# When the second layer's 64-bit weights are converted, and which engine rounds the second expert weights

## The chip, the cores and the metric

One core of one Trainium2 chip runs the whole program. The metric is the time of one execution in device microseconds (us). The engines that matter here are TensorE (PE: matrix products and transposes), VectorE (DVE), ScalarE (ACT), GpSimd (POOL) and SyncE (SP), which issues nearly all transfers. Each engine works through its own instructions strictly in the order in which the program lists them; they meet only through semaphores.

## The reference

```python
attn_out = _attn_ref(q, k, v)               # 2 x 8 heads, 1152 keys, queries averaged in pairs
x = attn_out.transpose(0, 2, 1, 3).reshape(1152, 512)
...
for e in range(8):                          # each token goes to one expert
    mask = expert_idx == e
    h = np.maximum(x[mask] @ w1[e], 0.0)    # 512 -> 1024
    out[mask] = gate_w[mask, None] * (h @ w2[e])
...
a = x @ w_a                                 # 512 -> 1536
b = x @ w_b
return (a * b @ w_out).astype(np.float32)
```

The arrays `w_a`, `w_b` and `w_out` of the last layer, the second layer, arrive as 64-bit floats; everything else is 32-bit. [...]

## The kernel before

The program has three stages: attention (to about 285 us), the experts (to about 466 us) and the second layer (to the end). For accuracy every matrix product is made of three: each operand is split into a high part (rounded to the matrix engine's format) and a low part (what the rounding left), and high x high, high x low and low x high are added.

**The expert stage** is a loop over steps m = 0 to 34. Steps 0 to 15 serve the first half of the tokens, 16 to 31 the second half; `ORDER` gives the sequence. A step handles a quarter of the hidden units of one expert slot; a slot has one tile of 128 tokens or two. In the second half the sequence is a a b a b a b b A A B A B A B B, where a and A have two tiles, b and B one. The one-tile steps are therefore 18, 20, 22, 23, 26, 28, 30 and 31. `moe_step(m)` writes into the queues, in this order: the evictions of what the PE made before (`x_ev`; `h_ev2(m-2)` for one-tile steps; `h_ev(m-1)`), the first product `s1(m)` on the PE, the transposes `h_tr(m-1)` of a one-tile step, the split of the first weights of the next step `split1(m+1)` (ACT makes `w1h`, DVE makes `w1l`), the split of the second weights `split2(m-1)` and `split2b(m-1)` (high part `w2h` by ACT where m-1 is in `W2_ACT`, else by DVE; the two halves of the low part `w2l` mostly by POOL), the second product `s2(m-2)`, and the loads of weights for later steps (SP, three buffers each for first and second weights). For a one-tile step the second product needs `hl`, the low part of the hidden values, which DVE writes in `h_ev2`: it stands in the DVE's queue at the head of the step in which the PE needs it.

**The second layer's weights** come in 18 pieces of 1 MB. `weights` and `convert` are a generator that each later step moves on by one stage. If a piece begins at step m, then SP loads `raw` at m; ACT makes `cvt` (`Abs`, line 1057) at m+3; DVE runs four instructions (lines 1059, 1060, 1061 and 1063) at m+4; ACT rounds it to `wh` and POOL makes the first half of `wl` at m+5; POOL makes the second half at m+6. These stand at the end of their step, behind `moe_step(m)`, and so in front of everything of step m+1. `raw` and `cvt` have two buffers each. `W_AT` lists the steps at which the first six pieces begin; they are called C1 to C6 here. `W_AT2` does the same for the other twelve, at later steps of the second layer. C1 and C2 are needed by the first product `f1(0)` of the second layer, which stands ahead of step 32 on the PE; C3 by `f2(0)`, C4 and C5 by `f1(2)`, C6 by `f2(2)`.

Before the change the DVE's four instructions of C1 to C6 stand at the ends of steps 23, 25, 28, 31, 32 and of the first round of the second layer. The attention's tiles are released before step 17, and the second layer's tiles (`raw` among them) take their place in the memory.

Of the kernel before, what the change touches and what calls it, by code (L numbers as in the profile page):

```python
# [42 lines left out]
SETUP_AT, ROUTE_AT = 26, 43  # L43
ROUND1, P2_AT, DS = 3, 4, (1, 2, 1, 2, 1)
CONV_LAG, Y_LAG = 3, 4
W_AT = (19, 21, 24, 27, 28, 31)
W_AT2 = range(3, 27, 2)
W2_ACT = (1, 2, 3, 4, 5, 6, 7, 8, 9, 10, 12, 13, 16, 17, 18, 19, 21, 22, 24, 25, 27, 28, 31)
Y_AT, YB_AT = 20, 34
XALL_AT = 53  # L50
ORDER = ('aabababbAABABABB', 'aabababbAABABABB')
# [8 lines left out]
def fused(ctx, tc, q, k, v, emb, tau, w1, w2, wa, wb, wo, out):  # L60
# [3 lines left out]
    def copy_hi(dst, src, engine=None):  # L64

        if engine is nc.vector:
            nc.vector.tensor_copy(dst, src)
        else:
            nc.scalar.activation(out=dst, in_=src, func=AF.Copy)  # L69

    def sub_lo(dst, src, hi, engine=None):

        (engine or nc.vector).tensor_tensor(out=dst, in0=src, in1=hi.bitcast(F32), op=ALU.subtract)  # L73
# [780 lines left out]
    def split2(m):  # L854
        w = M[m].pop("w2r")
        h, l = M[m]["w2"] = [moe.tile([P, 2, DM], F32R, name=f"w2{x}") for x in "hl"]
        copy_hi(h, w, None if m in W2_ACT else nc.vector)
        sub_lo(l[:, 0], w[:, 0], h[:, 0], nc.vector if m in W2_DVE[0] else nc.gpsimd)
# [227 lines left out]
    def advance(start):  # L1086
        if start and todo:
            running.append(weights(*todo.popleft()))
        for g in list(running):
            if next(g, "end") == "end":  # L1090
                running.remove(g)
# [35 lines left out]
    def drive():  # L1127

        if yq:
            moving.append(ytrans(*yq.popleft()))  # L1130
        for g in list(moving):
            if next(g, "end") == "end":
                moving.remove(g)
# [53 lines left out]
    while m < NM + 3:  # L1187
# [7 lines left out]
        if m >= Y_AT:  # L1195
            drive()
        advance(m in W_AT)
        m += 1
# [141 lines left out]
```

## Time and profile before

| | us |
|---|---|
| median of 3 runs | 700.35 (699.89 to 703.0) |
| the profiled execution | 699.06 |
| its span, first to last instruction | 697.4 |

| engine | busy us | share of the span |
|---|---|---|
| PE | 617.9 | 89% |
| DVE | 494.7 | 71% |
| ACT | 372.6 | 53% |
| POOL | 317.3 | 46% |

The mean granted clock of the PE over the execution is 0.945 of full speed. In the chain of work that ended last, PE has 49% of the span, DVE 20%, DMA 5%, ACT 4%, POOL 3%. The shares are averages over three stages with different limits; what a change in the expert stage is worth is read from that stage's own stretch.

### The profile page before, as it was taken

How to read it: one execution, taken by the hardware profiler on the slowest of the kernel's cores; microseconds unless marked ns; L12 is line 12 of the kernel's file. 1: busy time of each engine (PE TensorE's matmuls, PEld its weight loads, DVE VectorE, ACT ScalarE, POOL GpSimd, SP SyncE). 2: the span in 40 equal slices, each digit the busy share in tenths (PEclk: the TensorE clock that was granted, in tenths of full speed). 3: DMA queues.
4: the chain of work that ended last, by engine and by line, in shares of the span. 5: the costliest groups of instructions: out<-in, count | busy, mean ns of one | idle time of the engine just before them, and what ended most of it. 6: DMA issues, size and time to landing. Idle time of an engine off the chain costs nothing.

```text
span 697.4 us, 13210 instructions
## 1 busy us (share of the span) xinstructions
PE 617.9 (89%) x5253; PEld 555.6 (80%) x5253; DVE 494.7 (71%) x790; ACT 372.6 (53%) x512; POOL 317.3 (46%) x233
## 2 busy tenths in 40 slices
PE   8588979888976875998999988969999999999996
PEld 6477768777865765898888876859999999999995
DVE  4978989889899875458867598974445575665523
ACT  3868887987856664345546575435342324223210
POOL 3958878787665543233414567674011212212100
PEclk8879999999988796999999999989999999999999
DMA  8979899999886589995789987445011313211012
GB/s 285 267 176 225 212 210 238 209 238 226 191 220 153 139 196 235 270 332 188 249 270 302 360 305 246 164 143 174 1 60 61 121 61 106 77 62 60 1 46 94
DMA packets 210051, 125.04 MB, mean 179 GB/s; under 512 B 156216, under 2 KB 181816, under 8 KB 209984
## 3 DMA queue, kind: packets, MB, share of 16 engines
q1 hardware_dynamic: 208512, 119.41, 62.8%
q0 software_dynamic: 1472, 4.72, 1.9%
q8 instruction: 43, 0.70, 0.4%
q14 instruction: 24, 0.20, 0.1%
HBM read 72.11 MB, written 13.67 MB: 123 GB/s over the span
## 4 chain that ended last, share of the span: by engine, by line
PE 49%; DVE 20%; DMA 5%; ACT 4%; issue 4%; POOL 3%; SPq 0%; ACTq 0%; DVEq 0%; POOLq 0%
PE ps_s L1147 21%; DVE nm L377 4%; PE ps_s L872 4%; PE ps_o L1169 4%; PE ps_m L1169 3%; PE ps_y L1169 3%; PE ps_s L372 2%; PE ps_o L443 2%; DVE vl L260 2%; DMA w2r<-in_moe_w_dram 2%; DMA eT<-ehl 2%; POOL w2l L73 2%; PE ps_o L915 1%; DMA xr<-xbuf 1%; ACT ehl L394 1%
## 5 line engine op out<-in xcount | busy, mean ns | idle before, releaser
L403 POOL TENSOR_TENSOR ehl<-e,ehl 128x1152 f16<-128x1152 f32 x61 | 147.8, 2424 | 75.3 <-ACT ehl L394 33.9
L73 POOL TENSOR_TENSOR wl<-cvt,wh 128x512 fp32r<-128x512 f32 x36 | 50.5, 1420 | 147.9 <-ACT wh L69 144.3
L382 ACT ACTIVATE e<-ps_s,nm 128x1152 f32<-128x1152 f32 x72 | 87.8, 1220 | 38.4 <-DVE nm L377 28.8
L377 DVE TENSOR_REDUCE nm<-ps_s 128x1 f32<-128x1152 f32 x72 | 97.1, 1349 | 12.8 <-PE ps_s L372 12.5
L73 POOL TENSOR_TENSOR w2l<-w2r,w2h 128x512 fp32r<-128x512 f32 x42 | 63.7, 1532 | 91.3 <-ACT w2h L69 51.7
L372 PE MATMUL ps_s<-kTh,qT 64*128 64x512 f32 (+2 forms) x480 | 98.4, 399 | 2.5 <-issue 1.0
L443 PEld LDWEIGHTS <-eT 128*128 128x128 f16 x1944 | 78.3, 103 | 23.9 <-issue 12.9
L443 PE MATMUL ps_o<-vh,eT 128*128 128x65 f16 (+1 forms) x1278 | 82.0, 204 | 16.1 <-DVE x L466 10.3
L372 PEld LDWEIGHTS ps_s<-kTh,qT 64*128 64x128 f32 x480 | 74.2, 206 | 8.8 <-issue 2.4
L443 PE MATMUL ps_o<-vl,eT 128*128 128x65 f16 (+1 forms) x639 | 76.7, 204 | 0.0
L394 ACT ACTIVATE ehl<-e 128x1152 f16<-128x1152 f32 (+1 forms) x65 | 72.3, 1112 | 0.2 <-DMA eT<-ehl 0.2
L1157 DVE TENSOR_TENSOR asb<-ps_s,asb 128x384 f32<-128x384 f32 x36 | 19.9, 554 | 69.1 <-PE ps_s L1147 69.1
L69 ACT ACTIVATE abh<-asb 128x384 fp32r<-128x384 f32 x36 | 18.9, 524 | 83.0 <-DVE asb L1157 83.0
L1152 ACT ACTIVATE asb<-ps_s 128x384 f32<-128x384 f32 x36 | 17.8, 493 | 59.2 <-PE ps_s L1147 59.0
L372 PE MATMUL ps_s<-kTl,qT 64*128 64x512 f32 (+2 forms) x240 | 47.8, 366 | 1.1 <-DVE kTl L73 1.1
L73 DVE TENSOR_TENSOR w1l<-w1r,w1h 128x1024 fp32r<-128x1024 f32 x32 | 39.8, 1242 | 10.0 <-ACT w1h L69 9.5
L372 PEld LDWEIGHTS ps_s<-kTl,qT 64*128 64x128 f32 x240 | 44.2, 209 | 1.7 <-DVE kTl L73 1.7
L872 PE MATMUL ps_s<-xhi,w1l 128*128 128x256 f32 x128 | 38.6, 302 | 3.9 <-DVE w1l L73 3.9
L872 PE MATMUL ps_s<-xhi,w1h 128*128 128x256 f32 x128 | 39.2, 306 | 0.0
L872 PE MATMUL ps_s<-xlo,w1h 128*128 128x256 f32 x128 | 38.3, 299 | 0.0
L73 DVE TENSOR_TENSOR abl<-asb,abh 128x384 fp32r<-128x384 f32 x36 | 20.7, 574 | 24.5 <-ACT abh L69 24.5
L69 ACT ACTIVATE w1h<-w1r 128x1024 fp32r<-128x1024 f32 x32 | 34.0, 1061 | 5.1 <-DMA w1r<-in_moe_w_dram 5.1
(262 smaller groups left out, 1729.4 us busy)
## 6 DMA issues: line engine op xcount, KB each, us to landing
w1r<-in_moe_w_dram SPq DMA_DIRECT2D x32, 512.0 KB, 6.5
w2r<-in_moe_w_dram SPq DMA_DIRECT2D x32, 512.0 KB, 5.9
raw<-in_moe_w_a_dram SPq DMA_DIRECT2D x6, 1024.0 KB, 5.7
raw<-in_moe_w_b_dram SPq DMA_DIRECT2D x6, 1024.0 KB, 5.3
raw<-in_moe_w_out_dram SPq DMA_DIRECT2D x6, 1024.0 KB, 4.9
vs<-in_v_dram SPq DMA_DIRECT2D x8, 576.0 KB, 5.1
qs<-in_q_dram SPq DMA_DIRECT2D x16, 256.0 KB, 3.7
ks<-in_k_dram SPq DMA_DIRECT2D x7, 576.0 KB, 5.9
```

What stands on the lines that cost most here:

```text
L69: nc.scalar.activation(out=dst, in_=src, func=AF.Copy)
L73: (engine or nc.vector).tensor_tensor(out=dst, in0=src, in1=hi.bitcast(F32), op=ALU.subtract)
L372: nc.tensor.matmul(ps[:, c:c + n], qT[x][r:r + 64, o:o + 128], kT[y][r:r + 64, h, k0:k0 + n], start=i == 0, stop=i == len(ops) - 1)
L377: nc.vector.tensor_reduce(out=nm, in_=U[j]["ps"][:, 256:1408], axis=AX.X, op=ALU.max, negate=True)
L382: nc.scalar.activation(out=e, in_=U[j]["ps"][:, 256:1408], func=AF.Exp, bias=U[j]["nm"])
L394: nc.scalar.activation(out=ehl[:, 0, :c], in_=U[j]["e"][:, :c], func=AF.Copy)
L403: eng.tensor_tensor(out=ehl[:, 1], in0=U[j]["e"], in1=ehl[:, 0], op=ALU.subtract)
L443: nc.tensor.matmul(o, eT[:, 9 * x + n, :], v_[:, KEYS[n], :], start=(n == 0 and x == 0 and v_ is vh), stop=(n == 8 and x == 1))
L872: nc.tensor.matmul(p[:, 256 * j:256 * j + 256], a[:, kk, P * j:P * j + P], x[:, kk, :], start=(kk == 0 and x is xhi and a is w1h), stop=(k ...
L1147: nc.tensor.matmul(p[:, :384], w[:, kk, :], y[:, kk, :], start=(kk == 0 and x == 0), stop=(kk == 3 and x == 2))
L1157: nc.vector.tensor_tensor(out=ab, in0=F[n]["b"][:, :384], in1=ab, op=ALU.mult)
L1169: nc.tensor.matmul(F[n]["o"][t], a[:, P * t:P * t + P], w, start=(j == 0 and x == 0), stop=(j == 1 and x == 2))
```

## The change

Two constants differ. `W_AT` lets C1 to C6 begin at steps 17, 18, 22, 23, 27 and 28, where they began at 19, 21, 24, 27, 28 and 31: 2, 3, 2, 4, 1 and 3 steps sooner. Their loads, their ACT, DVE and POOL instructions all move with them. `W2_ACT` now holds every step from 16 on, so that the high parts of the second weights of steps 20, 23, 26, 29 and 30 are made by ACT; DVE made them before.

```diff
-W_AT = (19, 21, 24, 27, 28, 31)
+W_AT = (17, 18, 22, 23, 27, 28)
 W_AT2 = range(3, 27, 2)
-W2_ACT = (1, 2, 3, 4, 5, 6, 7, 8, 9, 10, 12, 13, 16, 17, 18, 19, 21, 22, 24, 25, 27, 28, 31)
+W2_ACT = (1, 2, 3, 4, 5, 6, 7, 8, 9, 10, 12, 13, *range(16, 32))
```

After it the DVE's instructions of C1 to C6 stand at the ends of steps 21, 22, 26, 27, 31 and 32.

## Rows read from the trace of the kernel before

**Rows 1.** Busy us by stretch: window, length, five engines (instructions), PE clock, DMA, GB/s.

```profile
476.00:690.00 214.00, 214.00 (x1146) 200.76 (x1145) 111.69 (x166) 69.24 (x115) 35.15 (x28) 1.00 0.19 64
```

**Rows 2.** PE timeline, 405 to 466 us: start, duration, instruction, [idle before].

```profile
409.75 0.50 PE L915 MATMUL ps_o<-w2h,hl 128*128 128x512 f32 x1 [2.27 <-DVE hl L73]
...
425.27 0.39 PE L872 MATMUL ps_s<-xhi,w1l 128*128 128x256 f32 x1 [3.42 <-DVE w1l L73]
...
443.37 0.39 PE L877 MATMUL ps_s<-w1l,xhi 128*128 128x256 f32 x1 [1.50 <-DVE w1l L73]
...
457.51 0.50 PE L915 MATMUL ps_o<-w2h,hl 128*128 128x512 f32 x1 [1.83 <-DVE hl L73]
...
464.34 0.80 PE L915 MATMUL ps_o<-w2h,hl 128*128 128x512 f32 x1 [5.08 <-DVE hl L73]
```

**Rows 3.** Chain of waits, 386 to 479 us: start, us, what ran.

```profile
387.95 1.39 PE ps_o L915 x6
389.33 2.87 PE ps_s L872 x24
...
425.27 4.35 PE ps_s L872 x22
...
464.34 2.08 PE ps_o L915 x4
466.42 6.12 PE ps_s L1147 x24
...
474.62 4.19 PE ps_s L1147 x24
```

**Rows 4.** Busy time by stretch: the stretch behind the longest wait of the PE.

```profile
465.00:470.00 5.00, 5.00 (x16) 4.72 (x15) 1.37 (x3) 2.10 (x4) 4.55 (x4) 0.50 0.41 125
```

**Rows 5.** Lines 1059, 1061 from 476 us: count: duration in ns, min/median/max, starts.

```profile
L1059 DVE TENSOR_SCALAR cvt<-cvt x12: 680/684/686, 508.8 to 647.5; 128x1024 f32<-128x1024 f32 x12
L1061 DVE SCALAR_TENSOR_TENSOR cvt<-raw,cvt x12: 1224/1226/1226, 510.3 to 649.0; 128x1024 uint32<-128x1024 uint32 x12
```

**Rows 6.** DVE timeline, 396 to 407 us.

```profile
396.27 0.69 DVE L73 TENSOR_TENSOR xlo<-ps_t,xhi 128x512 fp32r<-128x512 f32 x1 [3.69 <-ACT xhi L69]
...
403.51 3.33 DVE L1060 TENSOR_SCALAR cvt<-cvt 128x1024 uint32<-128x1024 uint32 x1
```

**Rows 7.** POOL timeline, 404 to 406 us.

```profile
403.73 2.54 POOL L73 TENSOR_TENSOR w2l<-w2r,w2h 128x512 fp32r<-128x512 f32 x2
```

**Rows 8.** DVE's groups, 388 to 464 us: count, busy us, mean ns, idle before.

```profile
L73 DVE TENSOR_TENSOR w1l<-w1r,w1h 128x1024 fp32r<-128x1024 f32 x11 | 14.1, 1279 | 1.4 <-ACT w1h L69 1.2
L1061 DVE SCALAR_TENSOR_TENSOR cvt<-raw,cvt 128x1024 uint32<-128x1024 uint32 x5 | 10.0, 1997 | 0.2
L1060 DVE TENSOR_SCALAR cvt<-cvt 128x1024 uint32<-128x1024 uint32 x5 | 10.0, 1996 | 0.2
L1063 DVE SCALAR_TENSOR_TENSOR cvt<-raw,cvt 128x1024 uint32<-128x1024 uint32 x5 | 8.1, 1611 | 0.2
L1059 DVE TENSOR_SCALAR cvt<-cvt 128x1024 f32<-128x1024 f32 x5 | 6.6, 1313 | 0.0
...
L67 DVE CAST w2h<-w2r 128x1024 fp32r<-128x1024 f32 x5 | 4.5, 903 | 0.0
```

**Rows 9.** ACT's groups, 372 to 476 us.

```profile
L69 ACT ACTIVATE w2h<-w2r 128x1024 fp32r<-128x1024 f32 x11 | 11.7, 1066 | 0.0
L1057 ACT ACTIVATE cvt<-raw 128x1024 f32<-128x1024 f32 x6 | 6.9, 1148 | 4.2 <-POOL wl L73 4.2
```

**Rows 10.** PE timeline, 397 us.

```profile
397.34 0.50 PE L915 MATMUL ps_o<-w2h,hl 128*128 128x512 f32 x1
```

**Rows 11.** SP timeline, 377 to 386 us: issues of transfers.

```profile
377.63 0.37 SPq L845 DMA_DIRECT2D w2r<-in_moe_w_dram  x1
...
385.61 0.38 SPq L1045 DMA_DIRECT2D raw<-in_moe_w_a_dram  x1
```

**Rows 12.** Busy time by stretch, DMA in the last two columns.

```profile
400.00:405.00 5.00, 5.00 (x32) 4.39 (x32) 4.01 (x4) 4.20 (x9) 4.83 (x5) 1.00 1.04 387
```

## The prediction

> **What bounds the kernel now.** I read the busy time by stretch first. From 476 us to 690 us the PE is busy for 214.00 of 214.00 us at the full granted clock [rows 1]: the second layer is products without a gap, and no conversion there can matter. So the change is worth what it does to the moment at which the PE gets there. Next I read the PE's timeline through the second half of the expert loop for its idle time. There are five long waits, all for DVE: 2.27, 3.42, 1.50, 1.83 and 5.08 us, together 14.1 [rows 2]; two waits for POOL, 0.5 together, I leave out. Then the chain of waits, for the clock. Behind the 3.42 us wait 22 matmuls take 4.35 us; at the 2.87 us that 24 take elsewhere they would need 2.63: 1.7 lost. Behind the 5.08 us wait four matmuls take 2.08 (six take 1.39, so four 0.93) and the next 24 take 6.12 where the same 24 later take 4.19: 3.1 lost [rows 3]. The granted clock there is 0.50, the lower of the two levels, 1.2 GHz [rows 4]. The waits of 2.27, 1.83 and 1.50 cost no clock. In all 14.1 + 1.7 + 3.1 = 18.9 us stand between this stretch and one that is bound by the PE alone; that is the most that can be won.
>
> Why DVE is late is plain from the queue: each long wait follows one of C1 to C5. Their DVE work stands at the ends of steps 23, 25, 28, 31 and 32, and the `hl` or `w1l` that the PE wants next stands right behind it.
>
> **The change part by part.**
> **Price of one conversion on DVE.** Undisturbed, the four instructions take twice 0.69 and twice 1.23, 3.83 us [rows 5] (one row of each pair of equal ones stands there). In the expert stage they average 1.31 + 2.00 + 2.00 + 1.61 = 6.92 [rows 8]. The surplus is POOL: one 0.69 us instruction of C1 took 3.33 while POOL ran two subtractions of together 2.54 [rows 6, 7], a surplus of 1.3 for each. Counted over C1 to C5, where about three subtractions lie beside each, it is 3.09 / 3 = 1.0. I take 1.3 for C1, 1.0 for the others.
> The Trainium skill (SBUF — State Buffer, Who interferes with whom) says that the port pair that DVE shares with GpSimd is locked for a whole instruction, and that ScalarE waits for nobody. By that, with a lock on every subtraction, each would cost its full 1.27 us and the sum below would be some 3 us higher, inside the range; the 3.33 us row agrees with it, the mean of the five doesn't.
>
> **The high parts that go to ACT.** Five casts leave DVE, 0.90 on average [rows 8], 4.5 us in all; ACT takes 1.07 each [rows 9], 5.3 us. ACT is busy for 53% of the span (first part of the page), and POOL and the PE get these high parts a step before the PE needs them, so I cost this at nothing on ACT. If that cover is gone, it is at most 1.07 a step. The gain is in the waits below, not beside them.
>
> **C6** came after the expert loop, where DVE had nothing that the PE waited for; now its 3.83 us and POOL's share lie inside it, in step 32. DVE's total in the loop is thus about what it was: 4.5 go, some 6.5 come. The question is only where the PE meets it.
>
> **The waits, one after the other.** PE prices: first product 2.87 with two tiles, half of that with one (half as many matmuls); second product 1.39 with one tile, twice that with two [rows 3]; transposes 0.4. DVE's `w1l` is 1.28 [rows 8], the small evictions 0.4 to 0.7 [rows 6].
> A (step 22). C1 now stands in step 21, where DVE was idle for 3.69 us [rows 6]. ACT's `Abs` of C1 in step 20 (1.15 us [rows 9]) pushes `w1h` and so `w1l` of step 22 back to about 392.3; C1 then takes 3.85 + 2.6 and ends at 398.7. `xlo` (0.6) and `hl` (0.4) follow: 399.7. The PE asks for that `hl` at 397.34 [rows 10]. Wait 2.4.
> B (step 23). Behind A the PE needs 0.9 + 0.4 and asks for `w1l` at 401.0; DVE has a second `hl` (0.6) and `w1l` to do, 401.6. Wait 0.6.
> C (step 24). C2 starts at 401.7, 3.85 + 2 for two subtractions: 407.5; then `xlo` and a `w1l` beside POOL, 409.8. The PE has 1.4 + 2.8 + 0.7 to do from 401.6 and asks at 406.6. Wait 3.2.
> Steps 25 to 27: no wait; DVE has no conversion in 23 to 25 and catches up, and waits for the PE in turn.
> D (step 28). From 409.8 the PE has about 20.4 us of products (steps 24 to 27) and asks for `w1l` at 430.2. DVE gets step 26's first work when `s2(23)` is done (418.9) and ACT has evicted (2.9 with `w1h`); `w1l`, a `w2l`, `yT0lo` (3.5) bring C3 to 425.3; 3.85 + 2 ends at 431.2, `w1l` at 432.3. Wait 2.1.
> E (step 28). C4 follows at 433.0 behind `yT0lo`. It meets the first half of C3's `wl` and both halves of `w2l`: 3.85 + 2.3, and `hl` at 439.6. The PE asks at 434.4 (1.4 + 0.5 behind 432.4). Wait 5.2, and as long a wait cost 3.1 of clock above, so 8.3.
> Steps 29 to 32: DVE waits for the PE. C5 starts at about 453 and meets only `hl` of step 30, which the PE wants behind `f1(0)` (4.19 us [rows 3]): no wait.
> F (step 33). C6 follows C5 at 460.0: 3.85 + 2.7, `hl` at 467.0; the PE asks at 463.5. Wait 3.5.
> Sum 2.4 + 0.6 + 3.2 + 2.1 + 8.3 + 3.5 = 20.1 against 18.9: 1.2 us more. The waits move; they don't go. Conversions in pairs of neighbouring steps give DVE some 14 us of work while the PE has 9, which is what makes E. Made against the profiled execution this is 699.06 + 1.2 = 700.3; the median of the runs is 1.3 above that execution, so I forecast 701.5.
>
> **Bounds of the unknown costs.** How many subtractions meet each conversion isn't in the trace of before. With one fewer at each (1.0 less, and 2 less in C and E, which stand behind two): A 1.4, B 0, C 1.2, D 1.1, E 3.2 + 1.7, F 2.5, sum 11.1, that is 7.8 less than before. With one more: 3.4, 0.6, 5.2 + 1.7, 3.1, 7.2 + 3.1, 4.5 + 3.1, sum 31.9, 13 more. My values lie nearer to the first, as the counts of before do.
>
> **The loads.** SP issues C1's load behind the second weights at 378.0 instead of 385.6 [rows 11], and C2's one step later, where it came two steps after C1's. Neither waits there: the memory of `raw` is free once step 16 is done. Behind them in SP's queue stand the weight loads of the next steps. While all sixteen DMA engines are busy 387 GB/s are moved [rows 12], so each MB makes what follows 2.7 us later. The weights of steps 22 to 24 are issued some 10 us before they are split, so I cost this at nothing. POOL's gathers of `yg` keep their places. The waits that SP had on `raw` at steps 28 and 31 go; nothing on the PE's path stood behind them.
>
> **The rivals.**
> Faster: DVE keeps pace. With the high parts on ACT, POOL's subtractions start earlier and are mostly done before a conversion begins, so that each meets one fewer. Against it: ACT stands still at `wh` until DVE ends, so POOL's work bunches behind it. The sum is the lower bound, 700.35 - 7.8 = 692.5.
> Slower: the clock. C and F (3.2 and 3.5 us) lie between the 2.27 us wait that left the clock alone and the 3.42 us wait that lost it. If both lose it, 1.7 and 3.1 us come on top: 701.5 + 4.8 = 706.3. It decides if C and F turn out like the longer of these two waits. Against it speaks only that both may come out shorter.
> The Trainium skill (TensorE: Matmul & The Clock Gate, HAM oscillation — how this bites in real kernels) has the same mechanism: a wait for data drops the clock, and the work behind it starts slow. The rows of before agree for the two longest waits.
> The loads: a weight tile of steps 22 to 24 comes 2.7 us late and the PE waits for it: 704.2.
> The change doesn't do what it says: a first load that finds its memory taken is held, and SP with it, so that C1 and C2 run as before. Then the waits of 2.27 and 3.42 with 1.7 of clock stand in for A to C (7.4 for 6.2): 702.7.
>
> **How the numbers follow.** Forecast 0.47, faster rival 0.2, clock 0.25, loads 0.05, held 0.03. A measurement of this kernel can tell about 0.5%, 3.5 us, from no change. The forecast and the held load lie within it, the clock and the loads are beyond it on the slow side, the first rival on the fast side: 0.2, 0.5 and 0.3. The range leaves out the outer part of the two larger rivals: 694.5 to 707.5. The forecast's own range is 697 to 705.
>
> **What would show it.** DVE idle only briefly ahead of step 22's `xlo`; PE waits for `hl` at about 397 and 434 us and none for `hl` in step 32; the longest wait in step 28, with a granted clock of 0.50 behind it; the product of 24 matmuls behind the last `hl` at 4.2 us (or 6.1 if the clock rival holds). I am wrong if the conversions come out at about 4 us each (too much POOL in the sum), if step 28 passes without a wait of 4 us or more, or if the weights' transfers end a PE wait.

## The result, and the profile after

The changed kernel takes 710.66 us (median of 4 runs, 708.84 to 714.16) against 700.12 us: a ratio of 1.0140, 95% interval 1.0100 to 1.0179. A second series of the same kernel on another occasion gave 1.0080 (1.0045 to 1.0116); the two intervals overlap from 1.010 to 1.012, about 7.5 us. It is slower, and by more than was forecast (701.5, range 694.5 to 707.5).

The profiled execution took 708.84 us with a span of 707.1 us, 9.7 more than before. The busy time by stretch (columns as in [rows 1]) shows that the second layer is untouched, 214.00 of 214.00 us as in [rows 1], and where the granted clock fell:

```profile
485.00:699.00 214.00, 214.00 (x1147) 200.84 (x1146) 111.17 (x166) 69.63 (x115) 32.39 (x26) 1.00 0.19 64
414.00:419.00 5.00, 4.43 (x22) 4.14 (x23) 2.75 (x3) 4.47 (x8) 2.76 (x2) 0.60 0.56 176
440.00:443.00 3.00, 3.00 (x16) 3.00 (x15) 2.93 (x3) 0.94 (x2) 2.58 (x2) 0.50 0.99 337
448.00:453.00 5.00, 5.00 (x26) 4.72 (x25) 4.66 (x4) 2.04 (x3) 4.44 (x3) 0.58 0.56 205
476.00:481.00 5.00, 5.00 (x20) 4.81 (x20) 1.69 (x1) 1.50 (x3) 4.11 (x5) 0.65 0.54 168
```

A measure is wanted that leaves out the stages ahead, which scatter: the first product of step 16, up to which all kernels here run the same program, begins anywhere from 363.9 to 370.9 us in their traces (366.2 before, 368.1 changed: 1.8 of the 9.7 us arise where nothing differs). I take the stretch from the first product of step 20 to the third product `f1(2)` of the second layer, where the PE becomes the bound. In the PE's timeline of the kernel before it runs between these two rows, 88.1 us:

```profile
386.35 0.28 PE L877 MATMUL ps_s<-w1h,xhi 128*128 128x256 f32 x1
...
474.46 0.33 PE L1147 MATMUL ps_s<-yT0hi,wh 128*128 128x384 f32 x1
```

In the changed kernel it is 95.7 us, 7.6 more, from the first to the last of these rows; between them are all waits of the PE in that stretch, and from 440.24 to 442.94 us the twelve matmuls of step 28's first product:

```profile
388.51 0.28 PE L877 MATMUL ps_s<-w1h,xhi 128*128 128x256 f32 x1
...
401.40 0.50 PE L915 MATMUL ps_o<-w2h,hl 128*128 128x512 f32 x1 [1.75 <-DVE hl L73]
...
403.55 0.39 PE L877 MATMUL ps_s<-w1l,xhi 128*128 128x256 f32 x1 [0.41 <-DVE w1l L73]
...
414.02 0.58 PE L872 MATMUL ps_s<-xlo,w1h 128*128 128x256 f32 x1 [5.83 <-DVE xlo L73]
...
415.15 0.58 PE L872 MATMUL ps_s<-xhi,w1l 128*128 128x256 f32 x1 [0.55 <-DVE w1l L73]
...
439.47 1.11 PE L1112 MATMUL ps_t<-ident,yg 128*128 128x128 f32 x4 [2.95 <-DVE yT0lo L73]
...
440.24 0.56 PE L877 MATMUL ps_s<-w1h,xhi 128*128 128x256 f32 x1
...
442.94 0.63 PE L915 MATMUL ps_o<-w2h,hh 128*128 128x512 f32 x1
...
447.06 0.79 PE L915 MATMUL ps_o<-w2h,hl 128*128 128x512 f32 x1 [3.07 <-DVE hl L73]
...
474.69 0.80 PE L915 MATMUL ps_o<-w2h,hl 128*128 128x512 f32 x1 [4.87 <-DVE hl L73]
...
484.17 0.33 PE L1147 MATMUL ps_s<-yT0hi,wh 128*128 128x384 f32 x1
```

They are 19.4 us where [rows 2] has 14.1, and once more all for DVE. The chain of waits shows the price of the clock behind them (what ran, and for how long):

```profile
405.96 6.16 DVE cvt L1061
...
415.15 4.16 PE ps_s L872 x22
...
447.06 2.07 PE ps_o L915 x4
449.14 4.25 PE ps_s L872 x24
...
474.69 2.08 PE ps_o L915 x4
476.77 5.48 PE ps_s L1147 x24
484.33 4.19 PE ps_s L1147 x24
```

At the prices of [rows 3] (2.63 for 22, 0.93 for four, 2.87 and 4.19 for 24) this is 1.5 + 1.1 + 1.4 + 1.2 + 1.3 = 6.5 us of clock, where before lost 4.8. Together 25.9 against 18.9: 7.0 of the 7.6 us. Both sums leave out smaller terms. The largest is the clock behind the wait of 2.95 us: it was granted at 0.50 there, and the twelve matmuls of step 28's first product took 2.70 us, where half of 2.87 is their usual price.

The first line of the chain is the surprise: one instruction of C2 took 6.15 us. Undisturbed it takes 1.23 [rows 5]. C2 on DVE's timeline, and POOL's for the same time:

```profile
403.42 1.78 DVE L1059 TENSOR_SCALAR cvt<-cvt 128x1024 f32<-128x1024 f32 x1
...
405.96 6.15 DVE L1061 SCALAR_TENSOR_TENSOR cvt<-raw,cvt 128x1024 uint32<-128x1024 uint32 x1
412.14 1.22 DVE L1063 SCALAR_TENSOR_TENSOR cvt<-raw,cvt 128x1024 uint32<-128x1024 uint32 x1
413.28 0.68 DVE L73 TENSOR_TENSOR xlo<-ps_t,xhi 128x512 fp32r<-128x512 f32 x1
```

```profile
406.06 1.29 POOL L73 TENSOR_TENSOR wl<-cvt,wh 128x512 fp32r<-128x512 f32 x1
407.31 2.49 POOL L73 TENSOR_TENSOR w2l<-w2r,w2h 128x512 fp32r<-128x512 f32 x2
409.76 1.25 POOL L73 TENSOR_TENSOR wl<-cvt,wh 128x512 fp32r<-128x512 f32 x1
```

POOL went through four subtractions in a row, from 406.06 to 411.01, at its undisturbed pace; DVE stood still for all four: 6.15 - 1.23 = 4.92, 1.23 for each. (The profile shows DVE as busy meanwhile; the instruction's length gives the lock away.) C2's first instruction took 1.78 for 0.69 us beside a fifth, so that C2 lost 6.0 us in all.

### The profile page after: what moved, and what is told of

Same layout as the page of the kernel before. It is cut to its first block, busy times and chain, and to the rows that moved or that the text cites. A ratio compares the mean times of both kernels' runs of the same rounds, so it can differ in the third digit from the quotient of the medians.

```text
span 707.1 us, 13203 instructions
## 1 busy us (share of the span) xinstructions
PE 619.3 (88%) x5253; PEld 557.3 (79%) x5253; DVE 496.1 (70%) x785; ACT 377.8 (53%) x517; POOL 317.8 (45%) x233
## 4 chain that ended last, share of the span: by engine, by line
PE 51%; DVE 22%; DMA 6%; issue 3%; ACT 2%; POOL 1%; SPq 0%; ACTq 0%; DVEq 0%
PE ps_s L1147 21%; PE ps_s L872 4%; DVE nm L377 4%; PE ps_o L1169 4%; PE ps_m L1169 3%; PE ps_y L1169 3%; DMA eT<-ehl 3%; PE ps_s L372 3%; PE ps_o L443 3%; DVE cvt L1061 2%; DVE vl L260 2%; PE ps_o L915 2%; PE ps_m L915 2%; PE ps_y L915 2%; DMA xr<-xbuf 1%
## 5 line engine op out<-in xcount | busy, mean ns | idle before, releaser
L443 PE MATMUL ps_o<-vh,eT 128*128 128x65 f16 (+1 forms) x1278 | 80.9, 203 | 16.1 <-DVE x L466 10.7
L372 PEld LDWEIGHTS ps_s<-kTh,qT 64*128 64x128 f32 x480 | 75.8, 210 | 7.0 <-issue 1.8
L69 ACT ACTIVATE abh<-asb 128x384 fp32r<-128x384 f32 x36 | 18.9, 525 | 82.5 <-DVE asb L1157 82.5
```

The costliest lines, as they stand in the source:

```text
L372: nc.tensor.matmul(ps[:, c:c + n], qT[x][r:r + 64, o:o + 128], kT[y][r:r + 64, h, k0:k0 + n], start=i == 0, stop=i == len(ops) - 1)
L443: nc.tensor.matmul(o, eT[:, 9 * x + n, :], v_[:, KEYS[n], :], start=(n == 0 and x == 0 and v_ is vh), stop=(n == 8 and x == 1))
```

## The experiments

The theory after the result: a conversion costs what DVE's queue holds back behind it, and POOL's subtractions beside it, each with up to its whole length; neighbouring conversions add up. The rivals are named with each run. The table has the steps at which C1 to C6 begin, the ratio to the kernel before with its 95% interval, and the stretch.

| kernel | begins | ratio | stretch, us |
|---|---|---|---|
| before | 19, 21, 24, 27, 28, 31 | 1 | 88.1 |
| changed | 17, 18, 22, 23, 27, 28 | 1.0140 (1.0100 to 1.0179) | 95.7 |
| changed again (e11) | same | 1.0080 (1.0045 to 1.0116) | 95.8 |
| only the beginnings (e1) | same | 1.0102 (1.0085 to 1.0119) | 95.2 |
| only the high parts (e2) | as before | 0.9981 (0.9961 to 1.0002) | 85.1 |
| only C1 and C2, and the high parts (e4) | 17, 18, 24, 27, 28, 31 | 1.0009 (0.9979 to 1.0038) | 88.3 |
| C4 a step later (e8) | 17, 18, 22, 24, 27, 28 | 1.0078 (1.0035 to 1.0121) | 92.5 |
| POOL relieved beside C2 (e6) | as changed | 1.0078 (1.0044 to 1.0112) | 93.2 |
| filler ahead of the last wait (e7) | as changed | 1.0101 (1.0061 to 1.0141) | 94.5 |
| spaced (e3) | 18, 21, 24, 26, 29, 31 | 0.9975 (0.9944 to 1.0006) | 85.6 |
| C5 apart (e9) | 19, 21, 24, 27, 29, 31 | 0.9935 (0.9898 to 0.9972) | 83.4 |
| one early, C5 apart (e10) | 17, 21, 24, 27, 29, 31 | 0.9859 (0.9816 to 0.9902) | 80.3 |
| e10 with `w2l` of step 24 on DVE (e12) | same | 0.9872 (0.9838 to 0.9905) | 80.3 |

All but "before" and e1 have the high parts of steps 16 on by ACT. The stretch comes from one trace of each kernel (two of the changed one). The ratios of e6, e7 and e8 lie within the interval of e11 and within each other's, so what these three show is in the waits of their traces and not in their times.

### The two halves of the change, and the first pair

```diff
 e1, only the beginnings
-W_AT = (19, 21, 24, 27, 28, 31)
+W_AT = (17, 18, 22, 23, 27, 28)
```

> Only the beginnings move (17, 18, 22, 23, 27, 28); the five high parts stay on DVE. Theory (DVE is late: where its conversions stand decides, and the casts add to DVE's queue in front of C1, C4 and C5): at least as slow as the changed kernel, 711 to 715 us, with waits of the PE for DVE in steps 22, 24, 28 and 33 as in the changed kernel, each up to 1 us longer. Rival (the high parts on ACT are the cause, since ACT stands still at wh behind DVE and POOL's low parts come late and bunched): the loss goes, 699 to 703 us.

```diff
 e2, only the high parts
-W2_ACT = (1, 2, 3, 4, 5, 6, 7, 8, 9, 10, 12, 13, 16, 17, 18, 19, 21, 22, 24, 25, 27, 28, 31)
+W2_ACT = (1, 2, 3, 4, 5, 6, 7, 8, 9, 10, 12, 13, *range(16, 32))
```

> Only the five high parts go to ACT; the conversions begin as in the kernel before. Theory: DVE loses the cast in front of C4 in step 31 (1.78 us in the trace of before), so the last wait for hl falls from 5.1 to 2.5 to 3.5 us; 695 to 699 us. Rival (ACT is the cause of the loss): 704 to 710 us, with POOL's w2l later and DVE's conversions longer.

```diff
 e4: as e2, and
-W_AT = (19, 21, 24, 27, 28, 31)
+W_AT = (17, 18, 24, 27, 28, 31)
```

> Of the beginnings only C1 and C2 move (17, 18); C3 to C6 begin as before (24, 27, 28, 31); the high parts are on ACT. Theory: the waits of steps 22 to 24 are those of the changed kernel (1.8, 0.4 and 6.4 us and 1.5 us of clock), in place of 2.3 and 3.4 with 1.7 of clock: about 2.5 us worse up to there; behind it the waits of before, with the last one 2 us shorter: 699 to 704 us. Rival (the pairs are harmless, and the loss is made in steps 27 to 33): 694 to 698 us.

The beginnings alone make the loss (95.2 us, ratio 1.0102); the rival that blames ACT falls. I had expected them to be at least as slow as the whole change, with each wait up to 1 us longer; they are about as slow, but with the five casts back on DVE the waits of steps 22 and 28 are longer (2.21 and 5.19 for 1.75 and 3.07 us), those of steps 24 and 27 shorter (4.54 + 0.55 and 1.48 for 6.38 and 2.95). The high parts alone shorten the stretch by 3.0 us; the ratio is just short of showing a gain, and its interval ends at 2.7 us. The gain isn't where I put it: the last wait stays at 5.08 us and the one in step 32 falls from 1.83 to 0.48, as the PE's timeline of e2 shows:

```profile
457.88 0.51 PE L915 MATMUL ps_o<-w2h,hl 128*128 128x512 f32 x1 [0.48 <-DVE hl L73]
...
464.71 0.79 PE L915 MATMUL ps_o<-w2h,hl 128*128 128x512 f32 x1 [5.08 <-DVE hl L73]
```

One of the 3.0 us isn't a wait at all: the 24 matmuls behind the last wait took 5.12 us here and 6.12 before, with the same 5.08 us ahead of them.

e4 differs from e2 in C1 and C2 alone and is 3.2 us longer; the changed kernel differs from e4 in C3 to C6 alone and is 7.3 us longer. So the 7.6 us are -3.0 (high parts) + 3.2 (first pair) + 7.3 (the others), each good to about 1 us, by which the clock behind equal waits differs from trace to trace. In e4 the same instruction of C2 took 6.15 us again, and the wait in step 24 was 5.82 + 0.55. The last wait stayed at 5.07 us, where I had expected 2 us less.

### The long instruction of C2

```diff
 e6: the changed kernel, and
-W2_DVE = ((2, 9, 10, 11, 12, 13, 14, 15, 19, 29), (2, 3, 5, 7, 9, 10, 11, 12, 16, 17, 25, 28))
+W2_DVE = ((2, 9, 10, 11, 12, 13, 14, 15, 19, 22, 29), (2, 3, 5, 7, 9, 10, 11, 12, 16, 17, 22, 25, 28))
```

> The changed kernel, but both halves of the second weights' low part of step 22 are made by DVE (behind C2 in its queue) and not by POOL beside C2. Theory (POOL's subtractions in a row lock DVE out: 6.15 us for one instruction of C2 with four of them beside it): with two of the four gone that instruction takes 3.5 to 3.9 us, the PE's wait in step 24 falls from 6.4 to 3 to 4 us with less or no clock lost; from the first product of step 20 to the third of the second layer 91.5 to 93.5 us where the changed kernel takes 95.7; 704 to 708 us. Rival (C2 is slow for another reason, its load or its inputs): that instruction stays at 6 us, and the added 1.4 us of DVE make it 710 to 713 us.

DVE's timeline of e6, and POOL's:

```profile
403.81 3.72 DVE L1061 SCALAR_TENSOR_TENSOR cvt<-raw,cvt 128x1024 uint32<-128x1024 uint32 x1
```

```profile
403.91 2.53 POOL L73 TENSOR_TENSOR wl<-cvt,wh 128x512 fp32r<-128x512 f32 x2
```

With two subtractions in place of four the instruction fell by 2.43 us, two times 1.2. The wait in step 24 went from 6.38 to 3.92 us, the stretch from 95.7 to 93.2. That the lock by POOL makes the length is shown. I had expected less clock to be lost, or none: the clock fell behind the shorter wait as well (22 matmuls in 5.06 us, where the changed kernel took 4.16).

### The clock behind the last wait

```diff
 e7: the changed kernel, and ahead of step 33
+        if m == NM + 1:
+            warm(64)
         moe_step(m)
```

`warm` transposes the identity into a bank that nobody reads.

> The changed kernel with 64 transposes of the identity, whose result nobody reads, on the PE ahead of step 33, some 4 us of work that falls into the last long wait for hl (4.9 us). Theory (the wait itself is DVE's and stays; 2.7 us behind it are lost to the lower clock): hl comes at the same time, the four matmuls behind it take 0.9 us where they took 2.1 and the next product 4.2 where it took 5.7; 93 to 94 us over the stretch from the first product of step 20 where the changed kernel takes 95.7; 706.5 to 709 us. Rival (these matmuls are slow because they wait for operands one by one): their times stay as they are, 709 to 713 us.

The chain of waits of e7, and its clock:

```profile
467.30 1.39 PE ps_o L915 x6
468.69 5.47 PE ps_m L311 x64
474.16 1.46 PE ps_o L915 x6
475.62 4.19 PE ps_s L1147 x24
```

```profile
473.00:478.00 5.00, 5.00 (x35) 4.74 (x34) 2.75 (x4) 2.31 (x4) 2.96 (x3) 1.00 0.19 57
```

The 64 transposes took 5.47 us, somewhat more than the wait, so none was left; then six matmuls took 1.46 us and the 24 took 4.19, at full clock. The time from `f1(0)` to `f1(2)` fell from 20.7 to 19.0 us, though the filler itself came out about half a us too long. What I had called the clock behind the last wait is the clock. The whole stretch fell by 1.2 us only, as the steps ahead of it ran 0.6 us longer (behind the wait in step 24, which was the same, 22 matmuls took 5.07 us and not 4.16); I had expected 93 to 94.

### Neighbours apart

```diff
 e8: the changed kernel, and
-W_AT = (17, 18, 22, 23, 27, 28)
+W_AT = (17, 18, 22, 24, 27, 28)
```

> The changed kernel, but C4 begins at 24 and not at 23, so that its DVE work stands at the end of step 28 and C3 and C4 have a step between them. Theory (two neighbouring conversions make the waits of 3.0 and 3.1 us in steps 27 and 28 and 2.7 us of lost clock): both waits fall to 1 us or less together, a wait of 1 to 2.5 us for w1l in step 30 comes; 90 to 92.5 us over the stretch where the changed kernel takes 95.7; 702 to 706 us. Rival (the total of DVE's work decides): the wait of step 30 is as long as those two, 708 to 712 us.

The PE's timeline of e8:

```profile
436.39 0.90 PE L1112 MATMUL ps_t<-ident,yg 128*128 128x128 f32 x3 [2.82 <-DVE yT0lo L73]
...
448.74 0.39 PE L877 MATMUL ps_s<-w1l,xhi 128*128 128x256 f32 x1 [1.71 <-DVE w1l L73]
```

The wait in step 28 is gone with its clock, and 1.71 us in step 30 stand for it: 92.5 for 95.7 us. The wait in step 27 stayed, so it is C3's alone and not the pair's; half of that expectation was wrong. C4 left two things at once here, its neighbour C3 and its place in front of step 28's `hl`; which of the two made the wait, this run doesn't separate.

```diff
 e3: the high parts on ACT, and
-W_AT = (19, 21, 24, 27, 28, 31)
+W_AT = (18, 21, 24, 26, 29, 31)
```

> The conversions begin at 18, 21, 24, 26, 29 and 31, so that DVE's instructions stand at the ends of steps 22, 25, 28, 30, 33 and of the first round of the second layer: never two in neighbouring steps, and never in front of a one-tile second product; the high parts are on ACT. Theory: the waits for hl in steps 22, 24, 28, 32 and 33 are under 1 us each, and what is left is waits for w1l of 1 to 3 us; 686 to 694 us, faster than the kernel before. Rival (DVE's total work decides, not where it stands): 697 to 705 us.

A miss: no second product waits for DVE's `hl` any more, and yet only 2.5 us are won. ACT's timeline of e3, and the PE's:

```profile
459.11 1.06 ACT L69 ACTIVATE wh<-cvt 128x1024 fp32r<-128x1024 f32 x1 [7.71 <-DVE cvt L1063]
```

```profile
461.74 0.44 PE L897 MATMUL ps_t<-ident,hs 128*128 128x128 f32 x2 [2.45 <-ACT hs L890]
```

With C4 in step 30 its `wh` stands on ACT ahead of step 32; ACT stood still for 7.71 us behind C4, and the PE waited for `hs` behind it. What is queued behind a conversion isn't DVE's work alone.

```diff
 e9: the high parts on ACT, and
-W_AT = (19, 21, 24, 27, 28, 31)
+W_AT = (19, 21, 24, 27, 29, 31)
```

> The high parts on ACT, the beginnings as in the kernel before but C5 at 29 and not at 28, so that no conversion stands in front of the last hl; C5 stands in step 33 behind it. Theory: the wait of 5.1 us for the last hl and the clock lost behind it go; f2(0) then waits 1 to 3 us for DVE, which does C5 first; 79.5 to 82.5 us over the stretch where the kernel with only the high parts moved takes 85.1; 693 to 698 us, faster than the kernel before. Rival (ACT stands still at wh of C4 in front of the last hh, as it stood in the spaced kernel): 84 to 87 us, 698 to 702 us.

The PE's timeline of e9:

```profile
454.49 0.50 PE L915 MATMUL ps_o<-w2h,hl 128*128 128x512 f32 x1 [0.46 <-DVE hl L73]
...
456.52 0.50 PE L915 MATMUL ps_o<-w2h,hh 128*128 128x512 f32 x1 [0.83 <-ACT hh L69]
...
464.16 0.50 PE L1169 MATMUL ps_o<-wh,abh 128*128 128x512 f32 x1 [1.80 <-ACT abh L69]
```

One conversion one step later than in e2: the last wait goes from 5.08 us for DVE's `hl` to 0.83 for ACT's `hh`, and 1.80 us in front of `f2(0)` come. There C5 now holds DVE until 461.5 us, and `abh` stands on ACT behind C5's `wh` and C6's `Abs` until 463.6. The stretch, 83.4 us, is a little over what I expected; the interval of the ratio, 0.9935, lies below 1.

### One conversion early

```diff
 e10: as e9, and
-W_AT = (19, 21, 24, 27, 29, 31)
+W_AT = (17, 21, 24, 27, 29, 31)
```

> The kernel with C5 apart (19, 21, 24, 27, 29, 31, high parts on ACT) but with C1 at 17, so that its DVE work fills the idle time of step 21 and no other conversion stands near it. Theory (a conversion costs by what stands behind it and by POOL's subtractions beside it): the wait of 3.2 us in step 24 becomes 1.8 and 0.4 us in steps 22 and 23; C2 meets two subtractions and not four, so the wait of 3.4 us and the 1.7 us of clock in step 27 become 1 to 2.5 us without clock; 79 to 81.5 us from the first product of step 20 to the third of the second layer, where the kernel with C5 apart takes 83.4; 0.985 to 0.991 of the kernel before. Rival (C1 in step 21 costs what the changed kernel showed there, 2.2 us on top): 84 to 86 us, 0.993 to 0.998.

The PE's timeline of e10:

```profile
404.87 0.50 PE L915 MATMUL ps_o<-w2h,hl 128*128 128x512 f32 x1 [1.74 <-DVE hl L73]
...
407.03 0.39 PE L877 MATMUL ps_s<-w1l,xhi 128*128 128x256 f32 x1 [0.41 <-DVE w1l L73]
...
428.79 0.39 PE L872 MATMUL ps_s<-xhi,w1l 128*128 128x256 f32 x1 [2.74 <-DVE w1l L73]
```

The total is as expected: 80.3 us and a ratio of 0.9859, 1.4% faster than the kernel before and, with e12, the fastest here. In part that is luck: C2 lost 3.0 us, three subtractions and not two, and the wait in step 27, 2.74 us, cost 1.4 us of clock where I had expected none. C1 in the idle time of step 21 is worth having when C2 isn't its neighbour.

```diff
 e12: as e10, and
-W2_DVE = ((2, 9, 10, 11, 12, 13, 14, 15, 19, 29), (2, 3, 5, 7, 9, 10, 11, 12, 16, 17, 25, 28))
+W2_DVE = ((2, 9, 10, 11, 12, 13, 14, 15, 19, 24, 29), (2, 3, 5, 7, 9, 10, 11, 12, 16, 17, 24, 25, 28))
```

> The kernel with one early conversion, and both halves of the second weights' low part of step 24 made by DVE in front of C2, not by POOL beside it. Theory (a subtraction of POOL costs a conversion 1.0 to 1.2 us, DVE makes it in 0.6 to 0.7 itself): C2 shrinks by some 2 us and begins 1.2 us later, so the wait for w1l in step 27 falls by 0.5 to 1 us; 78.5 to 81 us over the stretch. Rival (moved work is moved work): no shorter than the kernel with one early conversion.

The wait in step 27 fell from 2.74 to 1.97 us, as the theory had it; but the 22 matmuls behind it took 4.41 us (4.04 in e10), and the stretch is no shorter, as the rival had it. (In e10 some clock falls just behind the stretch: `f1(2)` took 5.13 us there and 4.21 in e12. The ratios don't tell the two apart.) The PE's timeline of e12 and the stretch behind it:

```profile
425.48 0.50 PE L872 MATMUL ps_s<-xhi,w1l 128*128 128x256 f32 x1 [1.97 <-DVE w1l L73]
```

```profile
425.00:430.00 5.00, 4.52 (x25) 4.52 (x26) 5.00 (x5) 3.50 (x5) 4.55 (x3) 0.66 0.73 226
```

### The changed kernel again

> The changed kernel once more, for its interval and a second trace. Theory (the whole loss is made between the first product of step 20 and the third of the second layer; what the first runs show beyond it is scatter of the stages ahead): 1.009 to 1.013 of the kernel before, 94.5 to 96.5 us over that stretch. Rival (the change also costs something in the stages ahead): 1.014 to 1.018.

95.8 us over the stretch, with every wait within 0.05 us of the first trace. The ratio, 1.0080, is a little under what I expected and clearly not the rival's. The loss is made in this stretch; what the first series shows beyond 7.6 us fits the scatter of the stages ahead.

## Why the prediction was wrong

The frame held: the second layer is bound by the PE, the change is worth what it does to the PE's waits in the expert loop, and these move and don't go. The sum was 20.1 us and came out at 25.9. Of the 5.8 us that it was short, C with its clock makes 4.7 and F with its clock 3.8; D adds 0.9, and A, B and E came out 3.5 below.

- **A, B (2.4 and 0.6):** 1.75 and 0.41. Right, with two subtractions beside C1 as counted; they cost 1.0 each and not the 1.3 that I took.
- **C (3.2):** 6.38, and 1.5 of clock behind it. This is the step that failed: "3.85 + 2 for two subtractions". C2 lost 6.0 us and not 2. Four subtractions stood beside its third instruction, `w2l` of step 22 and both halves of C1's `wl`, since a conversion shortly ahead brings its own `wl` along; and each cost 1.23 us and not 1.0, a mean that I had from conversions at which DVE and POOL took turns. The end of a fifth cost 1.1. e6 took two of the four away and got their price back. The trace of before could have told the count: there too C1's two `wl` stand beside C2, and its four instructions lost 4.0 us:

```profile
415.07 1.77 DVE L1059 TENSOR_SCALAR cvt<-cvt 128x1024 f32<-128x1024 f32 x1
416.88 1.67 DVE L1060 TENSOR_SCALAR cvt<-cvt 128x1024 uint32<-128x1024 uint32 x1
418.58 2.20 DVE L1061 SCALAR_TENSOR_TENSOR cvt<-raw,cvt 128x1024 uint32<-128x1024 uint32 x1
420.81 2.19 DVE L1063 SCALAR_TENSOR_TENSOR cvt<-raw,cvt 128x1024 uint32<-128x1024 uint32 x1
```

- **The weighing of the lock** on the port pair belongs to this. I let the mean of the five conversions speak against a lock on the whole instruction; at C2 each subtraction held DVE for its whole length, four times in a row. The Trainium skill (SBUF — State Buffer, Who interferes with whom) states the lock: whoever issues first has the shared pair for the whole instruction, and the other is blocked. The trace agrees at C2, with 1.23 us a subtraction; at C1, where the two engines took turns, each cost 1.0.
- **D (2.1):** 2.95, but another thing waits: the transposes of `yg` for a free bank, which `yT0lo` behind C3 gives, and not the first product for `w1l`. I hadn't priced the two buffers of `ps_t`.
- **E (5.2 + 3.1):** 3.07 + 2.5. In its place and smaller, though C4 lost 3.4 us to POOL and not 2.3: the clock had already fallen behind D, so that the PE reached `hl` later. That clock, 1.3 us on the first product alone, I hadn't priced. e8 shows that the wait goes when C4 moves a step away from C3 and from that `hl`.
- **F (3.5):** 4.87, and 2.4 of clock. C6 met POOL's subtractions nearly throughout and lost 3.6 us, where I had 2.7; this is read from the trace, no run took them away.
- **No wait in step 32, and none for loads:** right.
- **The clock rival:** it came true at both places that it named, for 1.5 + 2.4 = 3.9 us where I had priced 4.8. I gave it 0.25 because a wait of 2.27 us had left the clock alone; F came out longer than that, and C longer than any wait of before. I had also misread my own number: F's 3.5 us don't lie between 2.27 and 3.42 but above both, so that by my own comparison F's clock belonged into the sum. The sum put it at nothing without a reason.

A, B, D and E together were 13.4 and came out at 10.7; C and F with their clock were 6.7 and came out at 15.2. The mechanism was right, and two terms were mis-sized: what POOL's subtractions cost C2 and C6, and the clock behind C and F, which the sum put at nothing. My upper bound allowed one subtraction more at each, and 31.9 in all; the range was cut well short of that, although C2 of before had lost twice what I gave it.

Of the high parts I had written that the gain "is in the waits below, not beside them". Alone they are worth 3.0 us in the one trace of e2, and at most 2.7 by its ratio. On the new beginnings they are worth nothing (95.2 and 95.7): what they win in steps 22 and 28 is lost in steps 24 and 27.

## What to carry to other kernels

A block of work put at the end of a step costs what stands behind it in its own queue, and in the queue of every engine that waits for its result in order; find for each place the first thing that the critical engine wants, and prefer the places where that is late anyway. Do not put two such blocks close behind each other: the second meets the first one's follow-up work on the engine that can hold it up (here POOL; it cost C2 4.0 us two steps behind C1, and 6.0 in the next step). When a price is a mean over cases in which two engines take turns, count the instructions that can stand in a row and use their full length as the other end.

## What the runs showed of the hardware

POOL's subtractions and DVE's conversions, the instructions with one operand (0.69 us, lines 1059 and 1060) among them, take turns in some places: DVE's 0.69 and 1.23 us instructions then take 1.7 and 2.2, POOL's 1.25 us subtraction 1.7. In others POOL goes through two or four in a row while DVE stands still for 2.5 or 4.9 us. What decides between the two stays open.

The length of a wait alone doesn't tell whether the granted clock falls. Behind 1.97 us in step 27 of e12 it was 0.66 over 5 us, while behind the 2.27 us wait in step 24 of the kernel before it stayed at 1.00. e2 and e9 are the same program up to step 27: behind the wait in step 24, 3.22 us in e2 and 3.23 in e9, the clock over the next 5 us was 0.66 in e2 and 1.00 in e9:

```profile
413.00:418.00 5.00, 4.91 (x24) 4.63 (x25) 3.95 (x6) 4.58 (x7) 3.05 (x2) 0.66 0.63 217
```

```profile
410.00:415.00 5.00, 4.98 (x37) 4.47 (x36) 4.45 (x6) 4.32 (x8) 2.99 (x2) 1.00 0.70 226
```
